# Fewer zero matmuls ahead of the first products of a fused attention and expert kernel

## The chip, the cores and the metric

The kernel runs on one core of a Trainium2 chip. Its engines are TensorE (PE in the profile, with its weight loads as PEld), VectorE (DVE), ScalarE (ACT), GpSimd (POOL) and SyncE (SP), which issues most of the DMAs. The metric is the time of one execution on the device in microseconds (us); a kernel is judged by the median of its runs.

## The reference

Two stages are computed for 8 batches, 8 heads, 576 tokens and a head dimension of 64. The first is a linear attention with a norm; the second routes every token to 2 of 4 attention experts.

```python
kv  = einsum('bhsd,bhse->bhde', k, v)
out = einsum('bhsd,bhde->bhse', q, kv)
x   = out / sqrt(mean(out*out, -1) + 1e-6) * g_norm      # then heads side by side: (8, 576, 512)

logits = x @ w_gate; topk = the 2 largest of 4; w = softmax over the two
for e in range(4):
    q, k, v = x @ wq[e], x @ wk[e], x @ wv[e]
    a  = softmax(causal(q @ k.T / 8))
    ye = a @ v @ wo[e]
    out += (gate of e) * ye
```

## The kernel before

Every batch (a "block" b from 0 to 7) goes through the same steps, and each step is a small function with a short name: loads `lk`, `lv`, `lq`; the product of k and v (`kv`, line 414) into a PSUM bank; its copy to SBUF (`kvc`) and the copies of it with partitions exchanged (`kvx`); the 32x32 transposes of q on VectorE (`qc`, line 437); the product with q (`o`, line 450); squares and their sums (`sq`, `ms`, line 482); the norm (`ln`, `rs`, `na`, `nb`, `lo`), which is spread by matmuls (`bc`, line 563) and multiplied in (`xm`, line 571). The projections (`kp`, `qp`, line 643, and `v`, line 624), the scores (`sc`, line 674), their exponentials, the product with v (`pv`, line 719) and the output (`y`, line 794) follow. Expert weights arrive in fp32 stages (`lw`, line 374) and are scaled by `ws` (line 387) before use.

The order of all steps of all batches is written out by hand in the string `ORDER`, and the engine of each in `ENGINE`. Every engine works through its own steps in that order, and waits only for data and for buffers.

Loads are issued by SyncE in that order too. From batch 2 on, a load of k, v or q also waits until the load issued four places before it has landed (`FLIGHT = 4`, in `queued`).

In block 0 the steps up to the norm are done in two halves: heads 4 to 7 first (`kv` for chunks 2 and 3, `o` of half 1), then heads 0 to 3. Ahead of four of these steps stand zero matmuls: `zero_matmuls` (line 836) multiplies a 128x128 tile of zeros by itself in fp32 and writes into columns 256 to 383 of a bank that the step itself will use. The results aren't read. How many there are stands in a dictionary:

```python
ZEROS = {
    ("kv", 0, 2): 26, ("o", 0, 1): 9, ("kv", 0, 0): 4, ("o", 0, 0): 4,
}
```

So TensorE does, in this order: 26 zero matmuls, `kv` of chunks 2 and 3, 9 zero matmuls, `o` of half 1, 4 zero matmuls, `kv` of chunks 0 and 1, the sums of half 1, 4 zero matmuls, `o` of half 0. The first 26 need only the tile of zeros, which VectorE writes at the start. The profile shows each fp32 matmul as two records, so 26 zero matmuls are 52 records.

Of the kernel before, what the change touches and what calls it, by code (L numbers as in the profile page):

```python
# [23 lines left out]


ZEROS = {
    ("kv", 0, 2): 26, ("o", 0, 1): 9, ("kv", 0, 0): 4, ("o", 0, 0): 4,
}

ORDER = (  # L30
# [844 lines left out]
```

## Time and profile before

| | us |
|---|---|
| median of 3 runs | 205.02 (203.74 to 207.45) |
| the profiled execution, its own time | 206.06 |
| span of the profiled execution, first to last instruction | 204.4 |
| TensorE busy with matmuls | 191.1 (94%) |
| weight loads busy | 155.5 (76%) |
| VectorE busy | 135.9 (66%) |
| ScalarE busy | 129.7 (63%) |
| GpSimd busy | 70.6 (35%) |
| DMA traffic | 40.31 MB, 197 GB/s over the span |

In the rows of the trace the first number is the start in us from the first instruction, the second the length of the group; then come the engine, the line of the kernel, the operation, what is written from what is read, the shape, and how many records the group has. In brackets stands how long the engine had been idle before it, and what ended that.

### The profile page before, as it was taken

What the parts mean: (1) busy time and instruction counts of PE and PEld (TensorE: products, weight loads), DVE (VectorE), ACT (ScalarE), POOL (GpSimd) and SP (SyncE); (2) the same over time, 40 slices, a digit from 0 to 9 for tenths busy, and PEclk for the clock granted to TensorE, in tenths of its full rate; (3) what the DMA queues carried; (4) which work ended last, traced back from release to release, by engine and by line L of the source; (5) the groups of instructions that cost most, each with busy time, mean ns of one, the idle gap of its engine ahead of it and who ended that gap; (6) DMA issues with size and microseconds to landing.
All of it is one profiled execution on the core that took longest, in us unless ns stands there. A gap on an engine that the chain in (4) does not pass through costs nothing.

```text
span 204.4 us, 7128 instructions
## 1 busy us (share of the span) xinstructions
PE 191.1 (94%) x2943; PEld 155.5 (76%) x2960; DVE 135.9 (66%) x336; ACT 129.7 (63%) x240; POOL 70.6 (35%) x185
## 2 busy tenths in 40 slices
PE   7999899999999889999999999999999999999980
PEld 7976575788787568869878697888967878988740
DVE  7046799969446756766695557765877596667640
ACT  2035536749767268963875978887376647567961
POOL 8101354004355131408163552165126224126500
PEclk9999999999999999999999999999999999999999
DMA  4899997898986998785089960100043134026486
GB/s 151 267 363 354 334 226 196 275 343 247 272 275 213 301 291 310 220 281 192 5 238 337 288 236 3 55 3 0 3 154 145 62 114 152 2 89 205 168 326 195
DMA packets 33808, 40.31 MB, mean 197 GB/s; under 512 B 8288, under 2 KB 24944, under 8 KB 33776
## 3 DMA queue, kind: packets, MB, share of 16 engines
q1 hardware_dynamic: 33248, 39.20, 60.6%
q10 hardware_dynamic: 432, 0.66, 0.9%
q8 instruction: 23, 0.38, 0.8%
q14 instruction: 9, 0.07, 0.1%
q0 software_dynamic: 96, 0.01, 0.1%
HBM read 30.42 MB, written 9.44 MB: 195 GB/s over the span
## 4 chain that ended last, share of the span: by engine, by line
PE 63%; DMA 21%; DVE 5%; ACT 5%; issue 3%; ACTq 0%; POOL 0%; DVEq 0%; SPq 0%; POOLq 0%
PE banks L643 10%; PE banks L450 7%; PE banks L674 7%; DMA k_b<-in_k_dram 7%; DMA q_b<-in_q_dram 6%; PE banks L836 6%; PE banks L624 6%; PE banks L414 6%; PE banks L719 6%; PE banks L482 5%; PE banks L794 5%; DMA v_b<-in_v_dram 5%; DMA out_dram<-stage 4%; PE banks L563 2%; PE banks L762 2%
## 5 line engine op out<-in xcount | busy, mean ns | idle before, releaser
L686 ACT ACTIVATE PT<-banks 128x1024 bf16<-128x1024 f32 (+1 forms) x64 | 51.7, 835 | 11.9 <-PE banks L674 10.2
L693 POOL TENSOR_SCALAR_AFFINE_SELECT PT<-PT 128x256 bf16<-128x256 bf16 (+1 forms) x80 | 29.1, 386 | 20.6 <-ACT PT L686 20.3
L437 DVE STREAM_TRANSPOSE qT<-q_b 128x576 f32<-128x576 f32 x32 | 23.7, 758 | 8.5 <-DMA q_b<-in_q_dram 6.2
L571 DVE TENSOR_TENSOR xT<-banks,ob 128x576 fp32r<-128x576 f32 x32 | 23.4, 746 | 4.1 <-PE banks L563 3.8
L624 PE MATMUL banks<-wv_r,xT 128*128 128x256 f32 x160 | 24.5, 291 | 0.0
L643 PE MATMUL banks<-xT,wk_r 128*128 128x288 f32 x128 | 22.3, 307 | 0.1
L624 PEld LDWEIGHTS banks<-wv_r,xT 128*128 128x128 f32 x160 | 21.2, 189 | 1.4 <-DVE wv_r L387 0.2
L643 PE MATMUL banks<-xT,wq_r 128*128 128x288 f32 x128 | 22.1, 305 | 0.1
L414 PE MATMUL banks<-v_b,k_b 128*64 128x64 f32 x640 | 21.3, 224 | 0.9 <-DMA k_b<-in_k_dram 0.5
L414 PEld LDWEIGHTS banks<-v_b,k_b 128*64 128x64 f32 x640 | 19.7, 138 | 3.1 <-issue 0.9
L674 PE MATMUL banks<-qTp,kT 64*128 64x192 f32 (+3 forms) x224 | 21.3, 307 | 0.4 <-DVE xT L571 0.3
L674 PEld LDWEIGHTS banks<-qTp,kT 64*128 64x128 f32 x224 | 15.8, 185 | 6.0 <-issue 2.0
L643 PEld LDWEIGHTS banks<-xT,wk_r 128*128 128x128 f32 x128 | 18.4, 188 | 1.8 <-ACT ob L311 0.5
L643 PEld LDWEIGHTS banks<-xT,wq_r 128*128 128x128 f32 x128 | 18.3, 188 | 1.9 <-DVE kT L312 0.5
L450 PE MATMUL banks<-qT,kvs 32*64 32x288 f32 x256 | 19.0, 410 | 0.4 <-DVE g_den L608 0.3
L719 PEld LDWEIGHTS <-PT 128*128 128x128 bf16 x480 | 15.9, 97 | 4.5 <-issue 1.5
L474 POOL TENSOR_TENSOR sqs<-ob 128x576 f32<-128x576 f32 x14 | 16.1, 1156 | 7.7 <-DVE ob L312 4.9
L719 PE MATMUL banks<-vext,PT 128*128 128x65 bf16 x480 | 17.5, 193 | 1.0 <-issue 1.0
L450 PE MATMUL banks<-qT,kvm 32*64 32x288 f32 x256 | 18.2, 410 | 0.0
L794 PE MATMUL banks<-wo_b,OT 128*128 128x512 bf16 (+1 forms) x57 | 16.5, 372 | 1.8 <-issue 1.0
L311 ACT COPY stage<-banks 128x512 f32<-128x512 f32 x25 | 14.3, 593 | 5.8 <-PE banks L794 3.4
L311 ACT COPY ob<-banks 128x576 f32<-128x576 f32 x19 | 11.8, 637 | 8.2 <-PE banks L450 8.2
(95 smaller groups left out, 305.9 us busy)
## 6 DMA issues: line engine op xcount, KB each, us to landing
q_b<-in_q_dram SPq DMA_DIRECT2D x16, 576.0 KB, 6.2
out_dram<-stage SPq DMA_DIRECT2D x29, 256.0 KB, 2.6
v_b<-in_v_dram SPq DMA_DIRECT2D x16, 320.0 KB, 5.4
k_b<-in_k_dram SPq DMA_DIRECT2D x16, 320.0 KB, 4.8
v_b<-in_v_dram SPq DMA_DIRECT2D x16, 256.0 KB, 5.0
k_b<-in_k_dram SPq DMA_DIRECT2D x16, 256.0 KB, 5.2
out_dram<-stage SPq DMA_DIRECT2D x9, 128.0 KB, 2.4
stage<-in_moe_wk_dram SPq DMA_DIRECT2D x2, 256.0 KB, 7.3
```

What stands on the lines that cost most here:

```text
L311: return nc.scalar.copy(dst, src)
L414: use(nc.tensor.matmul(p_kv[hh * Dh : (hh + 1) * Dh, c, :], lhsT=k_t(b)[:, h, j, :], rhs=v_t(b)[:, h, j, :], start=(j == 0), stop=(j == LO ...
L437: nc.vector.transpose(q_part(b, dh)[:, ms].rearrange("p m (t i) -> p m t i", t=RUN), q_t(b)[:, ms, :, dh * 32 : (dh + 1) * 32],)
L450: use(nc.tensor.matmul(bank(n)[at : at + Dh, 0:HALF], lhsT=(kvs if z == dh else kvm)[b % 2][pp, m], rhs=q_part(b, dh)[pp, m], start=(dh == ...
L571: use(nc.vector.tensor_tensor(out=xTs[b % 2][:, 0 : NCH * S].rearrange("p (n s) -> p n s", s=S)[:, cs, cols], in0=both(ns)[:, :, 0:HALF], ...
L624: use(nc.tensor.matmul(bank(n)[:, at : at + E * Hd], lhsT=blocks_of(xTs[b % 2], c)[:, i * P : (i + 1) * P], rhs=w_r["v"][:, c, :, :].rearr ...
L643: use(nc.tensor.matmul(bank(n)[:, 0:HALF], lhsT=w_r[nm][:, c, 2 * pr : 2 * pr + 2, :].rearrange("p e f -> p (e f)"), rhs=blocks_of(xTs[b % ...
L674: use(nc.tensor.matmul(bank(ns[el])[:, o : o + hi - lo], lhsT=kTs[(2 * b + pr) % 3][pp, kb * P : (kb + 1) * P], rhs=tiles["qTp", b, pr][pp ...
L686: use(nc.scalar.activation(PTs[(2 * b + pr) % 3][:, :, 512 * j : 512 * j + o], both(ns)[:, :, 0:o], ACTF.Exp, scale=scale), *ns)
L693: nc.gpsimd.affine_select(out=d, in_=d, compare_op=AluOpType.is_ge, fill=0.0, base=0, pattern=[[0, 2], [1, w]], channel_multiplier=-1,)
L719: use(nc.tensor.matmul(heads[el][:, k_ * W1 : (k_ + 1) * W1], lhsT=PT[:, el, col : col + P], rhs=vexts[b % 2][:, kb, 2 * pr + el, :], star ...
L794: use(nc.tensor.matmul(bank(n)[:, 0 : cols.stop - cols.start], lhsT=OT[:, pr, at : at + P], rhs=wo_b[:, pr, cols], start=(pr == 0), stop=( ...
```

## The change

Only the four counts are different: 20, 6, 2 and 2 zero matmuls stand where 26, 9, 4 and 4 stood. The order, the tiles, the engines and all operations that contribute to the output are the same.

```diff
 ZEROS = {
-    ("kv", 0, 2): 26, ("o", 0, 1): 9, ("kv", 0, 0): 4, ("o", 0, 0): 4,
+    ("kv", 0, 2): 20, ("o", 0, 1): 6, ("kv", 0, 0): 2, ("o", 0, 0): 2,
 }
```

## The prediction

> **What bounds the kernel now.** I read three views, in this order. The timeline of TensorE over the first 20 us shows where the zero matmuls (L836) stand and what follows them:
>
> ```profile
> 1.12 8.11 PE L836 MATMUL banks<-zeros 128*128 128x128 f32 x52 [1.12 <-DVE zeros L210]
> 9.16 1.39 PE L414 MATMUL banks<-v_b,k_b 128*64 128x64 f32 x40
> 10.91 2.27 PE L836 MATMUL banks<-zeros 128*128 128x128 f32 x18 [0.36 <-ACT kvs L311]
> 13.11 0.45 PE L450 MATMUL banks<-qT,kvs 32*64 32x288 f32 x1
> ...
> 14.27 1.16 PE L836 MATMUL banks<-zeros 128*128 128x128 f32 x8
> 15.36 1.39 PE L414 MATMUL banks<-v_b,k_b 128*64 128x64 f32 x40
> ...
> 18.86 0.45 PE L450 MATMUL banks<-qT,kvs 32*64 32x288 f32 x1
> ```
>
> None of the four steps behind zeros (9.16, 13.11, 15.36, 18.86) has a bracket: TensorE comes to each straight from the zeros. In the front, then, the zeros are in the way, unless data would have been late too.
>
> The second view is the chain that ended last, after the front:
>
> ```profile
> 33.00 4.51 DMA k_b<-in_k_dram
> ...
> 58.04 6.85 DMA q_b<-in_q_dram
> 64.91 3.59 DMA k_b<-in_k_dram
> ...
> 68.63 1.58 PE banks L414 x40
> ```
>
> From 33.00 to 68.50 it is a string of loads (k, k, q, v, v, q, k), each issued as the one before it in the string landed. TensorE stands at its end and waits for k:
>
> ```profile
> 68.63 1.58 PE L414 MATMUL banks<-v_b,k_b 128*64 128x64 f32 x40 [0.52 <-DMA k_b<-in_k_dram]
> ```
>
> So what TensorE wins in front passes 68.6 only as far as the load issued at 33.00 moves with it; else it becomes a longer wait in that bracket. The third view, the windows, shows what lies on either side (start and end, length, busy time and records of PE, PEld, DVE, ACT and POOL, granted clock, DMA share, GB/s):
>
> ```profile
> 33.00:68.60 35.60, 33.84 (x530) 26.97 (x529) 25.86 (x61) 24.52 (x44) 11.49 (x26) 1.00 0.88 268
> 68.60:204.40 135.80, 127.31 (x1971) 104.14 (x1988) 88.79 (x218) 92.70 (x173) 47.53 (x128) 1.00 0.48 160
> ```
>
> In the stretch of the load string the DMA engines are 0.88 busy; afterwards they are 0.48 busy and TensorE is busy for 127.31 of 135.80 us. From 68.6 on I let a shift pass to the end one for one.
>
> **The change, part by part.** It removes 6 + 3 + 2 + 2 = 13 zero matmuls, 26 records, and adds nothing. The price of a record comes from two rows above: 18 records take 2.27 us and 8 take 1.16, so ten more cost 1.11, or 0.111 each. The first zeros are dearer:
>
> ```profile
> 2.20:5.20 3.00, 3.00 (x16) 3.00 (x16) 1.00 0.88 267
> 5.70:8.70 3.00, 3.00 (x29) 3.00 (x28) 1.00 0.83 266
> ```
>
> These are zero matmuls alone, 16 records that touch the first 3 us and 29 the second. Without the two that reach in from before, that is 0.214 us a record early and 0.111 later. The column of the granted clock says 1.00 for both, but the early rate is that of half a clock. What is dropped comes off the end of each row of zeros, where the cheap ones stand: 26 x 0.111 = 2.9 us. That would be the gain if nothing else were late. What else is late is in the loads and in VectorE's rows:
>
> ```profile
> 2.97 0.62 SPq L332 DMA_DIRECT2D k_b<-in_k_dram  x1
> k_b<-in_k_dram SPq DMA_DIRECT2D x1, 256.0 KB, 5.4
> 10.30 1.44 DVE L437 STREAM_TRANSPOSE qT<-q_b 128x576 f32<-128x576 f32 x2 [4.88 <-DMA q_b<-in_q_dram]
> 11.77 0.47 DVE L312 COPY kvm<-kvs 32x128 f32<-32x128 f32 x2
> ```
>
> *First `kv`.* Without 12 records it could start at 9.16 - 1.34 = 7.8. Its last piece of k is issued at 2.97 and lands 5.4 later, at 8.37. So it starts at about 8.45: 0.7 earlier, and the other 0.6 become idle time.
>
> *First `o`.* The zeros then start 0.7 earlier, at 10.2, and are 6 records (0.67) fewer, so they would let it go at 11.7. But the q it needs lands at 10.30, whatever TensorE does; the two transposes and VectorE's copies of kvs behind them end at 11.77 + 0.47 = 12.24. So `o` starts at 12.3, 0.8 earlier.
>
> *Second `kv`.* Shifted by 0.8 and without 4 records (0.44) it starts at 14.1 instead of 15.36. Its last k:
>
> ```profile
> 6.24 1.50 SPq L332 DMA_DIRECT2D k_b<-in_k_dram  x1
> k_b<-in_k_dram SPq DMA_DIRECT2D x1, 256.0 KB, 7.7
> ```
>
> This lands at 13.94, in time by 0.2. Lead 1.26.
>
> *Second `o`.* 18.86 - 1.26 - 0.44 = 17.16, a lead of 1.7. It needs two more transposes of q:
>
> ```profile
> 15.90 1.44 DVE L437 STREAM_TRANSPOSE qT<-q_b 128x576 f32<-128x576 f32 x2
> ```
>
> They ended at 17.34 and follow a copy on VectorE that comes 0.8 earlier with the first `o`. If they come earlier by as little as 0.2, the lead stays 1.7; if not at all, it is 1.5.
>
> So of 2.9 us, 1.2 turn into idle time (0.6 before the first `kv`, 0.6 before the first `o`), and block 0 goes on 1.7 earlier. Up to 33 us the lead meets two more covers. GpSimd scales half of wk:
>
> ```profile
> 23.64 3.19 POOL L387 TENSOR_SCALAR wk_r<-stage,g_part 128x256 fp32r<-128x256 f32 x3 [5.82 <-DMA stage<-in_moe_wk_dram]
> 28.27 1.29 PE L643 MATMUL banks<-xT,wk_r 128*128 128x288 f32 x8
> ```
>
> It starts as its DMA lands and ends at 26.83; the first projection would be due at 28.27 - 1.7 = 26.57, so the lead is cut there to about 1.4. The other is the load string. What starts it is on SyncE:
>
> ```profile
> 28.65 2.09 SPq L332 DMA_DIRECT2D v_b<-in_v_dram  x1
> 31.83 0.37 SPq L374 DMA_DIRECT2D stage<-in_moe_wq_dram  x1
> 32.30 2.00 SPq L332 DMA_DIRECT2D k_b<-in_k_dram  x3
> 30.75 1.05 DVE L387 TENSOR_SCALAR wk_r<-stage,g_part 128x256 fp32r<-128x256 f32 x3
> 27.28 0.57 SPq L374 DMA_DIRECT2D stage<-in_moe_wv_dram  x1
> stage<-in_moe_wv_dram SPq DMA_DIRECT2D x1, 256.0 KB, 5.3
> ```
>
> SyncE had its load of v out at 28.65 + 2.09 = 30.74, but the load of wq behind it went at 31.83, 0.03 after VectorE had scaled the second half of wk (30.75 + 1.05 = 31.80) and so let its stage go. With the lead of 1.4 that scaling ends near 30.4, so wq is issued as SyncE comes free, at 30.8, 1.0 earlier. Behind it stand three loads of k, from 32.30; the second of them, at 33.00, is the first of the string. By `FLIGHT` it must wait for the second load of wv, issued at 27.28, which lands 5.3 later: at 32.6. That landing doesn't depend on the front: the stage it fills was let go by GpSimd at 26.83. So the string can start at 32.6 instead of 33.00: **0.4 us** arrive, and the rest of the lead, 1.0, ends as wait before 68.6. The bounds are 0 (the string holds its pace by other landings, the DMA engines being 0.88 busy in it) and 1.7 (it moves with its engines). I take 0.4, since it stands on the rows of the string's own first issue.
>
> One rule of the Trainium skill bears on the dear records, in "TensorE: Matmul & The Clock Gate", Part 1: TensorE runs at half clock until about 3.4 us of activity have passed, and the window is free-running, so the moment differs between runs. Here the change of pace lies between 5.20 and 5.70, some 4.3 us after 1.12, which fits. By that rule a later window would make the zeros end later before the change and the lead before the first `kv` larger; the string would still start at 32.6, so the sum stays.
>
> The profiled execution took 206.06 us, 1.66 more than its span, and lies 1.04 above the median of 205.02. The sum gives 205.66 for its like, and 204.6 for the median.
>
> **The rivals.** *Nothing arrives.* The 0.4 is swallowed by the string, whose steps differ from 3.59 to 6.85 us; the bracket at 68.63 grows instead. For it: 0.88 DMA busy. Against it: the DMA engines have room just where the string begins (0.56 busy, 149 GB/s):
>
> ```profile
> 31.00:33.00 2.00, 2.00 (x38) 1.38 (x39) 1.89 (x5) 1.97 (x4) 1.22 (x1) 1.00 0.56 149
> ```
>
> Time: 205.0.
>
> *More arrives.* wq goes out 1.0 earlier, and with it the loads that count from it; if the string hangs on that one, 1.0 comes through, at the most the whole 1.7: 204.0 to 203.3.
>
> *The clock falls: slower.* The zeros keep TensorE occupied while it waits. Without 13 of them it idles for about 0.6 before 8.45, 0.36 before 10.2 and 0.6 before 12.3, some 1.6 us in 4.5. If that drops the clock, records cost 0.214 instead of 0.111 for a stretch like the 4.2 us at the start, in which 2.0 us are lost. One stretch eats the lead of 1.4 and leaves 0.6: the scaling of wk ends 0.6 later, and 205.6 results. Two stretches give +2.6, or 207.6; from three on (+4.6, 209.6) it is over 2%. It decides from the point at which idle time in some 3 us lowers the clock. Against it stands the stretch with about as much idle time in the front of this trace:
>
> ```profile
> 20.00:22.00 2.00, 1.06 (x14) 0.73 (x8) 1.55 (x4) 1.72 (x3) 0.00 (x0) 1.00 1.22 309
> ```
>
> TensorE was idle for 0.94 of 2 us, and the matmuls behind kept their pace (L414 x40 in 1.39 us at 9.16, at 15.36 and at 23.84). The Trainium skill has a rule on the side of this rival, on the same page, "A second HAM failure mode: psum-queue depth-cycling": frequent short idle times between groups of matmuls can make the clock swing. No row here shows that.
>
> ```profile
> 23.84 1.39 PE L414 MATMUL banks<-v_b,k_b 128*64 128x64 f32 x40
> ```
>
> **How the numbers follow.** The forecast of 204.6 has a chance of 0.42, nothing arrives 0.22, more arrives 0.13, one slow stretch 0.09, two 0.05, three or more 0.04, something unseen 0.05. The runs before spread from 203.74 to 207.45, that is from 1.3 below to 2.4 above their median, so 2% (4.1 us) is about what a measurement of this kernel can tell from no change. The range goes from 202.8 (the larger gain, 203.3, with some of the scatter) to 207.3 (no gain with the upper scatter, or nearly two slow stretches). Faster by over 2% would need 200.9, more than all the zeros removed are worth: 0.03, from the unseen. Slower by over 2% needs three slow stretches (0.04) or the unseen (0.02): 0.06. Within: 0.91.
>
> **What would show it.** Right: rows of zeros with 40, 12, 4 and 4 records; the first `kv` near 8.45 with a bracket that names k; the first `o` near 12.3 with a bracket that names VectorE; the second `o` near 17.2; the load of wq near 30.8; the next loads of k about 0.4 earlier; and a longer bracket at the `kv` near 68. Wrong: L414 x40 longer than 1.39 us in front (the clock), the string starting at 33.0 or before 32, or TensorE arriving at 68 without a wait for k.

## The result

| | before | after |
|---|---|---|
| median of 18 runs each | 205.11 us (203.74 to 207.78) | 203.56 us (201.77 to 205.85) |
| the profiled execution: span | 204.4 us | 201.4 us |

The ratio of after to before is 0.9931, with a 95% interval from 0.9903 to 0.9959: 1.4 us faster, 0.8 to 2.0. Two later sessions, on two chips, gave 0.9898 (0.9859 to 0.9937) and 0.9852 (0.9810 to 0.9894). The ratios leave slow executions out (4 of the 18 after), so they don't follow from the medians beside them.

The timeline of TensorE in the changed kernel, first 20 us (start, length, engine, line, operation, tiles, shape, records; in brackets the idle time before it and what ended it):

```profile
1.12 6.96 PE L836 MATMUL banks<-zeros 128*128 128x128 f32 x40 [1.12 <-DVE zeros L210]
9.28 1.39 PE L414 MATMUL banks<-v_b,k_b 128*64 128x64 f32 x40 [1.21 <-DMA k_b<-in_k_dram]
11.02 1.60 PE L836 MATMUL banks<-zeros 128*128 128x128 f32 x12 [0.35 <-ACT kvs L311]
...
13.71 0.71 PE L836 MATMUL banks<-zeros 128*128 128x128 f32 x4
14.36 1.39 PE L414 MATMUL banks<-v_b,k_b 128*64 128x64 f32 x40
15.67 1.16 PE L482 MATMUL banks<-sqs,ones 128*32 128x288 f32 x8
16.77 0.71 PE L836 MATMUL banks<-zeros 128*128 128x128 f32 x4
```

The first `kv` now waits for k, 1.21 us, as k lands later here than in the profile of before. From the second `kv` on (14.36 instead of 15.36) the front is ahead by 1.0 and more. How much of this is left later, and what comes to it, shows at two marks. The first is a wait of TensorE for VectorE (line 608) near 50 us, before and after:

```profile
50.62 0.45 PE L450 MATMUL banks<-qT,kvs 32*64 32x288 f32 x1 [0.32 <-DVE g_den L608]
```

```profile
49.50 0.45 PE L450 MATMUL banks<-qT,kvs 32*64 32x288 f32 x1 [0.31 <-DVE g_den L608]
```

So 1.12 are still there. The second is the string of loads, in the chain that ended last, with what follows it:

```profile
33.86 3.31 DMA k_b<-in_k_dram
...
63.40 3.67 DMA k_b<-in_k_dram
67.07 0.14 issue
67.21 1.39 PE banks L414 x40
```

TensorE gets its k at 67.21 instead of 68.63: 1.42 ahead. The span is 3.0 shorter, though. Most of the rest comes right behind, in the product with v (L719). Before:

```profile
72.27 1.06 PE L719 MATMUL banks<-vext,PT 128*128 128x65 bf16 x29
74.32 0.20 PE L719 MATMUL banks<-vext,PT 128*128 128x65 bf16 x1 [0.99 <-issue]
74.36 0.45 PE L762 MATMUL banks<-ident_b,osc 128*128 128x128 bf16 x5
```

After:

```profile
70.65 1.09 PE L719 MATMUL banks<-vext,PT 128*128 128x65 bf16 x30
71.58 0.44 PE L762 MATMUL banks<-ident_b,osc 128*128 128x128 bf16 x5
```

Before, TensorE stops for 0.99 us ahead of the last of 30 matmuls and nothing in the profile names a cause ("issue"). After, the 30 run through, and the transposes (L762) start 74.36 - 71.58 = 2.78 earlier. From there the distance stays to the end. The prediction had not spoken of that stop.

### The profile page after: what moved, and what is told of

Same layout as the page of the kernel before. It is cut to its first block, busy times and chain, and to the rows that moved or that the text cites. A ratio compares the mean times of both kernels' runs of the same rounds, so it can differ in the third digit from the quotient of the medians.

```text
span 201.4 us, 7076 instructions
## 1 busy us (share of the span) xinstructions
PE 187.7 (93%) x2917; PEld 152.7 (76%) x2934; DVE 136.1 (68%) x336; ACT 129.6 (64%) x240; POOL 70.1 (35%) x185
## 4 chain that ended last, share of the span: by engine, by line
PE 59%; DMA 25%; ACT 5%; DVE 3%; issue 3%; SPq 1%; POOL 1%; DVEq 0%; ACTq 0%; POOLq 0%
PE banks L643 10%; DMA k_b<-in_k_dram 9%; PE banks L674 7%; PE banks L414 6%; PE banks L450 6%; PE banks L624 6%; DMA q_b<-in_q_dram 6%; PE banks L719 6%; PE banks L794 6%; PE banks L482 5%; DMA v_b<-in_v_dram 5%; DMA out_dram<-stage 3%; DMA stage<-in_moe_wv_dram 3%; PE banks L563 3%; PE banks L762 2%
## 5 line engine op out<-in xcount | busy, mean ns | idle before, releaser
L719 PEld LDWEIGHTS <-PT 128*128 128x128 bf16 x480 | 15.8, 97 | 3.4 <-DVE ob L312 0.9
L311 ACT COPY stage<-banks 128x512 f32<-128x512 f32 x25 | 14.1, 593 | 5.3 <-PE banks L794 4.1
L719 PE MATMUL banks<-vext,PT 128*128 128x65 bf16 x480 | 17.4, 193 | 0.0
```

Source lines behind the costliest of these rows:

```text
L311: return nc.scalar.copy(dst, src)
L719: use(nc.tensor.matmul(heads[el][:, k_ * W1 : (k_ + 1) * W1], lhsT=PT[:, el, col : col + P], rhs=vexts[b % 2][:, kb, 2 * pr + el, :], star ...
```

## The experiments

Two theories stood against each other. **F**: the lead of the front is all, and it passes through. **S**: the stop is a late reload of TensorE's program, that is, its next instructions aren't there yet. The profile page has a queue of the kind "instruction":

```profile
q8 instruction: 23, 0.38, 0.8%
```

It counts 23 packets with 0.38 MB together, 16 KB each. One of them starts at 71.96 us, ahead of the stop, and ends at 72.90. From the start of the first packet to the start of the last TensorE begins 5500 records, matmuls and weight loads together, which is 250 for each packet: the queue keeps step with TensorE's program. If a reload falls due after a fixed number of instructions, then 13 zero matmuls fewer in front move the place in the program at which it falls due. "Program length" below means the number of instructions ahead of the stop: 43 zero matmuls before, 30 after. The edits are given in short form, most of them against the changed kernel.

**Both kernels once more.** No edit.

> The kernel before once more, to see what of its profile comes back. Theory F (the whole lead of the front reaches the end, the stall of 0.99 us at 73.33 was chance): ratio 1.00, and no stall of TensorE without a named cause near 73 us in this profile. Theory S (TensorE's next piece of program arrives late at a fixed place of its instruction stream): ratio 1.00, and the stall of about 1.0 us stands again in the product with v (L719) near 73 us.

> The changed kernel once more, beside the others on one chip. Both theories: ratio 0.993 (0.990 to 0.996), some 1.4 us faster. F: the rows of TensorE lead those of before by 1.1 to 1.5 us all the way from 20 us to the end. S: they lead by about 0.5 at 66 us and by 1.0 more behind the place of the stall, which isn't there.

Measured: 0.9988 (0.9950 to 1.0026) and 0.9898. The stop of the kernel before is back, at the same matmul:

```profile
50.69 0.45 PE L450 MATMUL banks<-qT,kvs 32*64 32x288 f32 x1 [0.32 <-DVE g_den L608]
70.74 1.06 PE L719 MATMUL banks<-vext,PT 128*128 128x65 bf16 x29
72.52 0.20 PE L719 MATMUL banks<-vext,PT 128*128 128x65 bf16 x1 [0.72 <-issue]
72.55 0.45 PE L762 MATMUL banks<-ident_b,osc 128*128 128x128 bf16 x5
```

This profile agrees with the first one of before until 50 us (50.69 and 50.62), but reaches L719 1.53 earlier, as it has no wait for k near 68 us. So the loads alone shift an unchanged kernel by 1.5 us between executions, and part of the 1.42 above may be that. In the repeated profile of after the lead is 1.77 at the mark near 50 us (48.85), the stop isn't there, and the span is 199.3. Against the repeated profile of before it leads by 1.84 at that mark, by 1.75 at the `kv` near 67 us and by 2.83 at L762 (69.72 against 72.55). S had asked for about 0.5 at 66 us and 1.0 more behind the stop: the second held (1.08), the first didn't.

**The time of the front kept, the program shorter: 13 wide matmuls.**

```diff
-    ("kv", 0, 2): 26,   # 128 columns each
+    ("kv", 0, 2): 13,   # 256 columns each; the others as before (9, 4, 4)
```

> The kernel before, but the first 26 zero matmuls of 128 columns are 13 of 256 columns: about the same time in front, 13 matmuls fewer in TensorE's program, as many as in the changed kernel. The sum of the zeros' time stays, so F gives ratio 1.00 (within 0.3%), about 205.1 us. S gives 0.994 to 0.996, about 1 us faster, with no stall near 73 us, since the place where the program is reloaded has moved as in the changed kernel.

Measured: 0.9979 (0.9951 to 1.0006), 204.15 us. The stop at L719 is gone, but another stands at an earlier place, and TensorE waits longer for k:

```profile
47.28 1.04 PE L674 MATMUL banks<-qTp,kT 64*128 64x64 f32 x12 [0.66 <-issue]
69.26 1.39 PE L414 MATMUL banks<-v_b,k_b 128*64 128x64 f32 x40 [1.36 <-DMA k_b<-in_k_dram]
```

The ratio is one that F had named, and missed what S had asked for; that the place of the stop moved fits S, not F.

**The time of the front short, the program as long as before: tiny matmuls.**

```diff
+        for _ in range(13 if n == ("kv", 0, 2) else 0):    # behind the first 20 of the changed kernel
+            matmul(bank(at)[0:32, 2 * P : 2 * P + 32], lhsT=zeros[:, 0:32], rhs=zeros[:, 0:32])
```

> The changed kernel with 13 tiny zero matmuls (32 x 32) behind the first 20, while TensorE waits for k: the front as short as in the changed kernel to within 0.6 us, TensorE's program as long as before. F gives 0.993 to 0.996, 203.6 to 204.3 us. S gives 0.998 to 1.000, about 204.6 us or more, with the stall of about 1 us back in the product with v near 72 us.

Measured: 0.9955 (0.9920 to 0.9990), 203.71 us, within what F had named; the stop is there, as S had it. The profile shows why the lead counts for little:

```profile
49.66 0.45 PE L450 MATMUL banks<-qT,kvs 32*64 32x288 f32 x1 [0.32 <-DVE g_den L608]
67.12 1.58 PE L414 MATMUL banks<-v_b,k_b 128*64 128x64 f32 x40 [1.08 <-DMA k_b<-in_k_dram]
70.76 1.06 PE L719 MATMUL banks<-vext,PT 128*128 128x65 bf16 x29
72.54 0.20 PE L719 MATMUL banks<-vext,PT 128*128 128x65 bf16 x1 [0.72 <-issue]
72.58 0.45 PE L762 MATMUL banks<-ident_b,osc 128*128 128x128 bf16 x5
```

At the mark near 50 us it leads the repeated profile of before by 1.03 (50.69 - 49.66). At L719 it leads by nothing (70.76 against 70.74): the 1.03 have become a wait of 1.08 for k.

**The same without the time of the tiny matmuls: 20 zeros cut into 33.**

```diff
+        few = 7 if n == ("kv", 0, 2) else count
+        for w in [P] * few + [P // 2] * (33 - few if n == ("kv", 0, 2) else 0):    # 7 whole, 26 of 64 x 64
```

> The changed kernel with its first 20 zero matmuls cut up into 7 whole ones and 26 of half the size (64 x 64): TensorE's program as long as in the kernel before, the time of the zeros as in the changed kernel (20 x 0.22 us), with no added time in front. Theory F (the lead of the front is all there is): 0.990 to 0.993 as the changed kernel, 203.0 to 203.6 us. Theory S (a reload of TensorE's program at a fixed place adds to it): 0.994 to 0.997, 204.0 to 204.5 us, with a stall of 0.7 to 1.0 us without a named cause in the product with v (L719) near 71 us.

Measured: 0.9979 (0.9931 to 1.0028), 205.12 us beside 205.98. The ratio lies outside both ranges, nearer to that of S. Its front is as early as that of the changed kernel, and its stop is the longest of all:

```profile
49.00 0.45 PE L450 MATMUL banks<-qT,kvs 32*64 32x288 f32 x1 [0.32 <-DVE g_den L608]
65.98 1.58 PE L414 MATMUL banks<-v_b,k_b 128*64 128x64 f32 x40 [0.58 <-DMA k_b<-in_k_dram]
71.95 0.20 PE L719 MATMUL banks<-vext,PT 128*128 128x65 bf16 x1 [1.26 <-issue]
```

F, which asked for the ratio of the changed kernel, is hard to hold after this: the same front gives 0.998 with the long program and 0.985 to 0.993 with the short one, though the intervals of 0.998 and 0.993 still overlap.

**One row of zeros, or the other three, shortened in time, with the program length of after.** Wide matmuls keep the time of the rows that aren't shortened.

```diff
 first:  ("kv", 0, 2): 20 of 128,             ("o", 0, 1): 3 of 128 + 3 of 256, then 2 of 256 and 2 of 256
 rest:   ("kv", 0, 2): 14 of 128 + 6 of 256,  ("o", 0, 1): 6 of 128,            then 2 of 128 and 2 of 128
```

> Only the first row of zeros is shortened in time (20 instead of 26). The other three keep their time of before (9, 4 and 4), but with as few instructions as in the changed kernel, by matmuls of 256 columns, so that the program is reloaded at the same places. By the prediction's steps the first kv wins 0 to 0.7 us, as k lands, and all of that goes on, as there is no other cover while the later zeros stand: the second o leads by 0 to 0.8. With the stall gone as well: S gives 0.994 to 0.998, F 0.996 to 1.000.

> Only the last three rows of zeros are shortened in time (6, 2, 2); the first keeps its 26 by 14 of 128 and 6 of 256 columns, so that the program is as long as in the changed kernel. By the prediction's steps the first o comes 0.67 earlier, the second kv 1.1 and the second o 1.55: nearly the whole lead of the changed kernel. F and S both: 0.990 to 0.994, as the changed kernel. If the first six matmuls are what matters, 0.997 to 1.000.

Measured: 0.9882 (0.9834 to 0.9931) and 0.9864 (0.9806 to 0.9921). The first gained more than either theory had asked for. In its one profile the front isn't early at all: k landed late (a wait of 1.71 before the first `kv`), and the mark near 50 us stands at 50.98, behind before. Neither profile has the stop at L719. Each part of the change thus gained about as much as the whole did in the other sessions, and what the two kernels share is the shorter program. In the second the front leads at that mark by 0.99 (49.63), and then its profile, of an execution of 205.41 us beside a median of 203.62, shows something else: a long wait for k, and after it the `kv` in 2.11 us instead of 1.39 and the granted clock at 0.50.

```profile
67.53 2.11 PE L414 MATMUL banks<-v_b,k_b 128*64 128x64 f32 x40 [1.50 <-DMA k_b<-in_k_dram]
```

**The program shorter still, the front exactly as before.** This is the run that decides between F and S.

```diff
-    26, 9, 4 and 4 of 128 columns
+    13 of 256, then 1 of 128 + 4 of 256, then 2 of 256 and 2 of 256
```

> The kernel before with the time of all its zeros kept, but by 22 matmuls, most of them of 256 columns, instead of 43: the front as late as before, TensorE's program 21 matmuls (84 instructions) shorter. Theory S: the stall in the product with v near 73 us isn't there, 0.990 to 0.996. Theory F: 0.998 to 1.002, as the front hasn't changed. As the shorter program of the run with 13 wide ones gave only 0.998 with a new stall of 0.66 us at 46.6 us, a ratio over 0.998 with other stalls in the profile would say that moving the reloads pays only by luck.

Measured: 0.9902 (0.9868 to 0.9935), 203.94 us beside 205.62.

```profile
50.61 0.45 PE L450 MATMUL banks<-qT,kvs 32*64 32x288 f32 x1 [0.32 <-DVE g_den L608]
70.62 1.09 PE L719 MATMUL banks<-vext,PT 128*128 128x65 bf16 x30
71.55 0.44 PE L762 MATMUL banks<-ident_b,osc 128*128 128x128 bf16 x5
```

Beside the repeated profile of before it is as late at 50 us (50.61 and 50.69) and at L719 (70.62 and 70.74), and 1.00 earlier at L762 (71.55 and 72.55), where the stop had been; the spans are 201.4 and 202.5. So a gain of 1.0% comes without any time won in front, beside the 1.5% of the changed kernel in the same session (0.9852, the intervals overlap). F, by which the lead of the front is all, falls. The stop is worth 0.7 to 1.3 us, and this ratio asks for 2.0 (1.3 to 2.7): where the rest of it comes from isn't shown.

**Loads that wait for the sixth load back.**

```diff
-FLIGHT = 4
+FLIGHT = 6
```

> The changed kernel with loads that wait for the sixth load back instead of the fourth. If the string of loads between 33 and 68 us holds TensorE up (the prediction's step), the k before 68 us lands earlier and the bracket at that kv goes: faster than the changed kernel by 0.5 us or more, 0.986 to 0.990 against before. If TensorE seldom waits for it: 0.990 to 0.994, as the changed kernel, or slower by crowded transfers.

> The changed kernel with loads that wait for the sixth load back, beside the changed kernel on one chip. If the string of loads still costs the changed kernel something, 0.3 to 0.8% below it: 0.983 to 0.988 against before. If not, the same as it.

> The changed kernel once more for comparison with the other three: 0.990 to 0.993 against before; no stall near 71 us in the product with v.

Measured: 0.9840 (0.9796 to 0.9885); then, beside the changed kernel on one chip, 0.9863 (0.9830 to 0.9895) against 0.9852 (0.9810 to 0.9894) for that, for which 0.990 to 0.993 had been expected. Neither of its profiles has a wait for k near 68 us. But it is not faster than the changed kernel by anything that this comparison can tell.

**No zeros behind the first row.**

```diff
+    ("kv", 0, 2): 10 of 128 and 20 of 64 x 64 (the time of 20), ("o", 0, 1): 0, ("kv", 0, 0): 0, ("o", 0, 0): 0
```

> The zeros of the first row as long as in the changed kernel (10 whole, 20 of half size), none ahead of the other three steps; 30 matmuls in all, so the program is as long as in the changed kernel. If the clock holds, the second o can start no earlier than its transposes of q end (16.9 to 17.3): the lead is that of the changed kernel or 0.3 us more, 0.987 to 0.993. If the idle time (about 2.2 us between 9.9 and 12.3) lowers the clock, matmuls behind it take twice as long for some us, the lead of the front is gone and 0.995 to 1.000 results.

Measured: 0.9889 (0.9841 to 0.9937). But the median of all its twelve executions is 204.91 us beside 205.62, only 0.3% less. In its profile the clock does fall (windows: busy time and records of PE, PEld, DVE, ACT, POOL, then the granted clock, DMA share, GB/s):

```profile
9.00:11.00 2.00, 0.82 (x28) 0.85 (x29) 0.00 (x0) 0.00 (x0) 0.00 (x0) 1.00 0.95 306
11.00:13.00 2.00, 0.84 (x20) 0.65 (x15) 1.36 (x2) 0.85 (x3) 0.00 (x0) 0.53 1.07 356
13.00:15.00 2.00, 1.77 (x32) 1.43 (x32) 0.52 (x3) 0.00 (x0) 0.00 (x0) 0.50 1.05 377
15.00:17.00 2.00, 2.00 (x43) 1.47 (x30) 0.64 (x1) 1.19 (x2) 0.00 (x0) 0.50 1.08 357
17.00:19.00 2.00, 2.00 (x27) 1.17 (x24) 1.97 (x4) 0.86 (x3) 0.56 (x2) 0.76 1.10 349
```

Each row is 2 us long, and 0.50 below full is half clock throughout, so the parts below 1.00 add up to 2 x 2 x (0.47 + 0.50 + 0.50 + 0.24) = 6.8 us at half clock. By the median that costs most of the gain, as had been expected for a clock that falls. The third profile of the changed kernel (an execution of 205.98 us beside a median of 203.23) has such a fall too, after a wait for k of 2.17 us:

```profile
9.40 1.39 PE L414 MATMUL banks<-v_b,k_b 128*64 128x64 f32 x40 [2.17 <-DMA k_b<-in_k_dram]
11.14 2.93 PE L836 MATMUL banks<-zeros 128*128 128x128 f32 x12 [0.35 <-ACT kvs L311]
```

Twelve zeros take 2.93 us there instead of 1.60, and the second `kv` starts at 15.89, later than before the change (15.36).

## Why the prediction was right or wrong

**The sign and the range were right; the size was not.** It was 0.4 to 0.5 us (204.6); measured are 1.4, or 1.55 between the medians. That 203.56 lies in the range says little for the mechanism: the range, 4.5 us wide for the scatter of the runs, held no gain at all as well.

**The steps in front** held in order and roughly in size. The rows of zeros have 40, 12, 4 and 4 records. The first `kv` hangs on k alone: 8.45 was forecast, 9.28 and, in the repeated profile, 8.20 are measured. The first `o` was forecast for 12.3 with a wait for VectorE; it came at 12.56 straight from the zeros, and in the repeated profile at 11.72 with a wait of 0.18 for VectorE. The second `kv` was forecast for 14.1 and came at 14.36, the load of wq for 30.8 and came at 30.64. The lead near 50 us was 1.12, 1.77 and, with the clock down, less than nothing (51.07 against 50.62); 1.4 was forecast for 32 us.

**That the string of loads swallows 1.0 of the lead** is the first step that failed. The repeated profiles, before and after, show a sign that the prediction had named for being wrong: TensorE comes to the `kv` without a wait for k.

```profile
67.10 1.58 PE L414 MATMUL banks<-v_b,k_b 128*64 128x64 f32 x40
```

```profile
65.35 1.39 PE L414 MATMUL banks<-v_b,k_b 128*64 128x64 f32 x40
```

The lead of 1.84 near 50 us is still 1.75 there. In the first pair of profiles, where TensorE waits 0.52 and 0.59 for k, the lead is 1.12 near 50 us and 1.42 at the `kv`. Only the run with tiny matmuls lost its 1.03 to a wait of 1.08. The one with 33 matmuls in the first row, beside the repeated profile of before, led by 1.69 near 50 us and by 1.12 at L719 (69.62 against 70.74); there its longer stop took half of that, and 0.56 were left at L762. The two runs with a short front and a long program gained 0.2% and 0.45%, which is 0.4 and 0.9 us, beside 0.4 forecast (the first interval includes no gain).

How I had derived the 0.4 was wrong as well. The load that was to go at 32.6 went at 33.86: it waits for the second load of wv, as derived, but that was issued at 28.06 instead of 27.28 and took 5.74. Before the change something else had held it, in a row ahead of those that the prediction shows of that chain:

```profile
32.11 0.89 PE banks L643 x5
33.00 4.51 DMA k_b<-in_k_dram
```

Though it began later, the string ended earlier after the change. Its pace differs by more than 0.4 us from one execution to the next, as the two profiles of before show.

**The other failed step is "from 68.6 on I let a shift pass to the end one for one".** The rows of before that I read past showed it: 0.99 us of "issue" at 73.33, in a product that otherwise hands over a matmul every 0.03 us. I took TensorE's program as free. The term that was left out is this stop, 0.7 to 1.3 us in the four profiles with the long program, and absent in all with a shorter one. The rival "more arrives" had the right time (203.3 to 204.0) and, by the repeated profiles, was right that the lead goes through. But the string did not start earlier with wq, as that rival had it, and the stop wasn't in it.

**The clock rival** is real, but not at the price or the place I gave it. In two of three profiles of the changed kernel the clock stays at 1.00; in the third it falls for 3.4 us in front and costs the lead, as forecast for one stretch. Averaged over an execution, the granted clock is below 0.990 in 9 of the 36 executions of the changed kernel and in 9 of the 69 of before that ran beside the experiments; these are too few to price it. It doesn't decide: over all executions the medians of the changed kernel are lower in each of the three sessions (by 1.55, 2.08 and 2.39 us).

**What S rests on.** Four profiles of three kernels with 43 zero matmuls (before twice, the tiny ones, the 20 cut into 33) stop at the same place in TensorE's program. Windows that end where they stop, in this order, with the records of PE and PEld in brackets:

```profile
0.00:73.33 73.33, 68.51 (x1105) 55.00 (x1105) 49.80 (x124) 39.06 (x73) 24.11 (x60) 1.00 0.90 273
```

```profile
0.00:71.80 71.80, 68.20 (x1105) 54.97 (x1105) 49.51 (x124) 39.09 (x73) 24.05 (x60) 1.00 0.91 280
```

```profile
0.00:71.83 71.83, 66.61 (x1105) 53.87 (x1105) 49.52 (x124) 39.07 (x73) 23.79 (x60) 1.00 0.91 278
```

```profile
0.00:70.68 70.68, 65.20 (x1105) 51.98 (x1105) 49.69 (x124) 39.06 (x73) 23.81 (x60) 1.00 0.92 281
```

All stop after 1105 matmul records and 1105 weight loads, though at times up to 2.65 us apart. The shorter programs of after and of the 13 wide matmuls have stops without a named cause elsewhere:

```profile
0.00:27.84 27.84, 23.63 (x345) 19.08 (x345) 17.56 (x51) 9.72 (x21) 9.49 (x28) 1.00 0.92 283
```

```profile
0.00:46.62 46.62, 43.32 (x597) 32.86 (x598) 32.17 (x85) 19.96 (x41) 12.79 (x33) 1.00 0.93 277
```

The distances are 597 - 345 = 252 and 1105 - 597 = 508 matmuls with about as many weight loads: 504 and 1016 records. The Trainium skill, "Perfetto Trace Analysis", The 4-stage abstract model, gives an instruction 64 bytes. By that, as an estimate, a packet of 16 KB holds 256 of them, and the distances are two and four packets less 8 each. TensorE's semaphore instructions, which the windows don't count, fill this up: between these matmuls the trace of before has 8 and 9 of them, and 252 + 252 + 8 = 512, 508 + 507 + 9 = 1024. So stops fall at places that are whole packets apart in TensorE's program.

The packets' own times in the traces tie the stops to the reload (q8, us from the start of the span):

| profile | packet | ends | TensorE stops | and goes on | packet to going on |
|---|---|---|---|---|---|
| before | 8th | 72.90 | 73.33 | 74.32 | 1.42 |
| before, repeated | 8th | 71.13 | 71.80 | 72.52 | 1.39 |
| tiny matmuls | 8th | 70.93 | 71.83 | 72.54 | 1.61 |
| 20 cut into 33 | 8th | 70.57 | 70.68 | 71.95 | 1.38 |
| after | 2nd | 26.83 | 27.84 | 28.26 | 1.43 |
| after, third | 2nd | 28.34 | 29.34 | 29.85 | 1.51 |
| 13 wide matmuls | 4th | 45.98 | 46.62 | 47.28 | 1.30 |

All stops end 1.30 to 1.61 us after the packet is in, whether TensorE had come to the place 0.1 or 1.0 us after it. No row names the packet as the cause, but the end of the stop keeps step with it, and not with TensorE's own arrival. In none of the 14 traces does TensorE pass one of the three places sooner than 1.26 us after its packet. In the ten with a shorter program its matmul 1106 comes 1.57 us or more after the eighth packet, as that count then falls on later work, and there is no stop. The changed kernel doesn't stop after 345 matmuls in its repeated profile as its second packet was in at 25.61, and TensorE came there 1.50 later. Not shown is why a packet comes when it does, nor what the 13 wide matmuls would have given without their own stop.

## What to carry to other kernels

Read the idle time called "issue" on TensorE before pricing anything ahead of it: it marks a place where the program itself may come late (a packet of the instruction queue then lands little more than 1 us before the engine goes on), and adding or dropping instructions far in front moves that place onto other work. To price a filler, change its time and its number of instructions separately, as with wider or smaller matmuls here. And before counting a lead through a string of loads, look at a second profile of the same kernel: here it moved by 1.5 us on its own.

## What the runs showed of the hardware that I had not expected

- TensorE stopped for 0.72 to 1.26 us at a fixed instruction of its program, in a stretch where a matmul with its weight load passes every 0.03 us (29 in 1.06 us with the end of the last). It went on 1.38 to 1.61 us after a packet of the instruction queue had landed. The same kernel with its zeros in 22 matmuls didn't stop there, and was 1.0% faster; with them in 30 it stopped elsewhere, and 0.2% was left.
- The granted clock fell to 0.50 after single waits of TensorE of 1.50 and 2.17 us (3.4 us long each time) and after 2.59 us followed by 1.39 us (6.8 us long). It stayed at 1.00 after waits of 1.21, 1.36, 1.54, 1.71 and 1.74 us, so the length of the wait alone doesn't decide. The Trainium skill, "TensorE: Matmul & The Clock Gate", Part 1, lets the clock fall after an idle window of some 3.4 us; here it fell after 1.50, less than half of that. The length of the low stretch, once or twice 3.4 us, agrees with its window.
- A zero matmul of 32 x 32 keeps the program as long at less time: 26 records of 32 x 32 took 1.01 us, against 0.111 us each for 128 x 128.
